# Gated attention and MLP for one token: the result in two PSUM banks, the MLP part added by matmul, one store, and the value products behind the second half of the scores

## The chip, the cores and the metric

The kernel runs on one core of a Trainium2 chip. Such a core has a matmul engine (TensorE, PE in the profile, with PEld for its weight loads), a vector engine (VectorE, DVE), a scalar engine (ScalarE, ACT), GpSimd (POOL) and SyncE (SP), which here issues most transfers. Matmuls write to PSUM; the other tiles lie in SBUF. The metric is the device time of one execution in microseconds, and kernels are compared by the median of several executions.

## The reference

One token for each of 8 sequences goes through a windowed attention over a cache (A) and an MLP (B), mixed by a gate per sequence:

```python
def _A_ref(x, k_cache, v_cache, wq, wo):            # x: 8 x 1 x 448
    W = 1024                                        # the last 1024 of 4096 positions
    q = (x @ wq) -> 8 x 16 heads x 1 x 256
    k, v = last W rows of 8 key/value heads, each used by 2 query heads
    p = softmax(q k^T / 16)
    return (p v).reshape(8, 1, 4096) @ wo           # wo: 4096 x 448
def _B_ref(x, w1, b1, w2, b2):
    return gelu(layernorm(x) @ w1 + b1) @ w2 + b2   # 448 -> 1792 -> 448
g = sigmoid((x * gate_w).sum(-1))                   # one number per sequence
return g * a + (1 - g) * b
```

Everything is bf16 in memory. Keys and values of the window are 33.5 MB each, and wo and wq 3.7 MB each; no part is read twice.

## The kernel before

The attention is cut into 16 units (`u`): one sequence and four of its eight key/value heads each, 2 MB of K and 2 MB of V. K and V of a unit, and the weights, come through a ring of nine SBUF slots. A list (`plan`) fixes the order of the loads: wq, K0, w1, w2, then K of a unit followed by V of two units before, last V14, V15 and the two halves of wo in ten pieces (`WO_PARTS`, L72, says how each of four quarters is cut). All of them are issued by SP in that order; `done` marks a slot as used and lets `pump` issue the next load into it.

The order of the work on each engine is the order in which the program is written (`manual_schedule`), so an instruction that waits holds up everything behind it on its engine. For a unit the steps are:

- `turn_keys` (L358, DVE, two halves): K is transposed in 32x32 blocks.
- `scores` (L424 and L430, PE, two halves): one masking matmul and eight matmuls into a PSUM tile `S`.
- `top` (L442, L444, DVE), `share` (L450, PE): the maximum, exchanged between the four heads.
- `expo` (L456 DVE, L459 ACT): exponentials `E` and their row sums.
- `turn` (L472, DVE): `E` transposed to `ET`. `total` (L483, PE) and `invert` (L493 DVE, L494 ACT): the inverse of the row sums.
- `values` (L502, PE): 16 matmuls of `ET` with V into `PO`, in four column groups, and a scaled copy of one half of `PO` on ACT (`first`, L511).
- `gather` (L517, DVE): the other half added, giving `os_`. `finish` (L532, PE): two f32 matmuls that transpose and normalise, and a copy into `oT` (L535, ACT).

The loop at L615 runs these steps for several units at once: in the round of unit `u` come the scores of `u`, the softmax of `u`-1, the value products of `u`-2 and the end of `u`-3. After the loop (L633 on) the remaining steps of the last units follow. `spread_rows` (L657 PE, L664 DVE) brings `oT` into the row order of wo, for two quarters at a time: the first two need units of the first heads, the others all units. `project` (L673) multiplies one quarter with wo: eight weight blocks, each used by three matmuls of 160, 144 and 144 output columns, which lie at partitions 0, 32 and 64 of one PSUM tile `A_ps`. `mlp_out` (L593 to L605) does the same for the MLP and leaves `(1 - g) * b` in `mixb` in that layout. At the end one DVE operation (L691) computes `g * a + mixb` for all three column parts, and three stores (L701) write them: two issued by SP and one by ACT.

Of the kernel before, what the change touches and what calls it, by code (L numbers as in the profile page):

```python
# [8 lines left out]
ACT = mybir.ActivationFunctionType  # L9
ALU = mybir.AluOpType  # L10
AXIS = mybir.AxisListType
BF16 = mybir.dt.bfloat16
F32 = mybir.dt.float32
# [5 lines left out]
def kernel(  # L19
# [15 lines left out]
    nc = tc.nc  # L35
    P = nc.NUM_PARTITIONS

    NB, Sq, D = A_x.shape
# [13 lines left out]
    NF = F // P  # L52
    FH = F // 2
    HH = HD // 2
    PAIR = 2
    OT = 4
    CUTS = (0, 160, 304, D)
    DO = CUTS[1]
    QN = 512
    QUAD = 4  # L60
    RQ = QUAD * rep
# [7 lines left out]
    HPQ = 4  # L69
    NHQ = Hq // HPQ  # L70
    NJ8 = HPQ * NJ
    WO_PARTS = [[(0, 4), (4, 8)]] * 2 + [[(0, 4), (4, 6), (6, 8)]] * 2  # L72
    RING = 9
    LAG = 2
    NK = 4
# [30 lines left out]
    def done(n=1):  # L106
        consumed[0] += n
        pump()
# [37 lines left out]
    def add_kv(name, src, u, parts=1):  # L146
        add((name, u), kv_loader(src, u, parts))
# [15 lines left out]
        if u >= LAG:  # L163
            add_kv("v", A_v_cache, u - LAG)
    for u in range(NQ - LAG, NQ):
        add_kv("v", A_v_cache, u)
    for q in range(0, NHQ, 2):
        add(
            ("wo", q),
# [9 lines left out]
    def slot(*key):  # L179
        return slots[index[key]]  # L180

    consts.tile([P, 304], BF16, name="pad")
    x_sb = consts.tile([NB, D], BF16)
    pump()
    nc.scalar.dma_start(x_sb[:], xf)
# [16 lines left out]

    NX = NR + 2

    def tiles(ps):
        return [
            (ps[32 * i : 32 * i + NB, 0 : c1 - c0], slice(c0, c1))
            for i, (c0, c1) in enumerate(zip(CUTS, CUTS[1:]))
        ]

    xz = consts.tile([NB, 2, P], BF16)
    yz = consts.tile([NB, 2, P], BF16)
    nc.vector.memset(xz[:], 0.0)
# [12 lines left out]
    place = consts.tile([P, CH, BLK], BF16)  # L226
    oT = consts.tile([P, Hq, NJ, NB], BF16)
    gg = consts.tile([NB, 2], F32)
    spread = consts.tile([NB, OT, P // OT], F32)
    gg_s = consts.tile([P, 2], F32)  # L230
    ones_r = consts.tile([1, NB], BF16)
    mixb = consts.tile([P, DO], F32)
    res = consts.tile([P, DO], BF16)
    nc.vector.memset(spread[:], 0.0)
    nc.vector.memset(ones_r[:], 1.0)

    def transposed(dst, src, srcz):
# [57 lines left out]
    def norm_and_gate():  # L295
        stats = consts.tile([NB, nc.vector.BN_STATS_DIM], F32)
        nc.vector.bn_stats(stats[:], x_sb[:])
        mv = consts.tile([NB, nc.vector.BN_AGGR_DIM], F32)
        nc.vector.bn_aggr(mv[:], stats[:])
        eps_t = consts.tile([NB, 1], F32)  # L300
        nc.vector.memset(eps_t[:], 1e-5)
        rstd = consts.tile([NB, 1], F32)
        nc.scalar.activation(rstd[:], mv[:, 1:2], ACT.Sqrt, bias=eps_t[:], scale=1.0)
        nc.vector.reciprocal(rstd[:], rstd[:])
        y_sb = consts.tile([NB, D], BF16)
        nc.vector.tensor_scalar(
            y_sb[:],
            x_sb[:],
            scalar1=mv[:, 0:1],
            scalar2=rstd[:],  # L310
            op0=ALU.subtract,
            op1=ALU.mult,
        )
        for h in range(2):
            nc.vector.tensor_copy(yz[:, h, h::2], y_sb[:, DM:D])
        transposed(yT, y_sb, yz)
        prod = consts.tile([NB, D], F32)
        gl = consts.tile([NB, 1], F32)
        nc.vector.scalar_tensor_tensor(
            prod[:],  # L320
            in0=x_sb[:],
            scalar=1.0,
            in1=gw_b[:],
            op0=ALU.mult,
            op1=ALU.mult,
            accum_out=gl[:],
        )
        gth = consts.tile([NB, 1], F32)
        nc.scalar.activation(gth[:], gl[:], ACT.Tanh, scale=0.5)
        nc.vector.tensor_scalar(  # L330
            gg[:, 0:1], gth[:], 0.5, 0.5, op0=ALU.mult, op1=ALU.add
        )
        nc.vector.tensor_scalar(
            gg[:, 1:2], gth[:], -0.5, 0.5, op0=ALU.mult, op1=ALU.add
        )
        nc.vector.tensor_copy(
            spread[:, :, 0:NB],
            ident[0:NB, 0:NB]
            .rearrange("p (o b) -> p o b", o=1)
            .to_broadcast([NB, OT, NB]),  # L340
        )
        gp = ps_misc.tile([P, 2], F32, tag="misc", name="gp")
        nc.tensor.matmul(  # L343
            gp[:],
            lhsT=spread[:].rearrange("p i b -> p (i b)"),
            rhs=gg[:],
            start=True,
            stop=True,
        )
        nc.vector.tensor_copy(gg_s[:], gp[:])  # L350

# [2 lines left out]
    def turn_keys(u, hf):  # L354
        kn = slot("k", u)
        kt = ktpool.tile([P, CH, NK, BLK, NPAR], BF16, tag="kt", name="kt")
        KT[u, hf] = kt
        nc.vector.transpose(  # L358
            kt[:].rearrange("p c k x r -> p (c k x r)").bitcast(WORD),
            kn[:, hf * CH * Dh : (hf + 1) * CH * Dh].bitcast(WORD),  # L360
        )
        if hf == NH - 1:
            done()
# [163 lines left out]
    def finish(u):  # L527
        b, half = divmod(u, Hkv // QUAD)
        os_, rs = soft.pop(u), rsel.pop(u)
        sm = ps_sm.tile([P, NJ, RQ], F32, tag="sm", name="fin")  # L530
        for j in range(NJ):
            nc.tensor.matmul(  # L532
                sm[:, j, :], lhsT=os_[:, j::NJ], rhs=rs[:], start=True, stop=True
            )
        nc.scalar.copy(  # L535
            oT[:, half * RQ : (half + 1) * RQ, :, b].rearrange("p h j -> p j h"), sm[:]
        )

    def mlp_hidden():
# [30 lines left out]
        )  # L570
        z2 = consts.tile([P, NF, NB], F32)
        nc.vector.tensor_tensor(z2[:], z[:], z[:], op=ALU.mult)
        uu = consts.tile([P, NF, NB], F32)
        nc.vector.tensor_scalar(
            uu[:], z2[:], 0.044715, 1.0, op0=ALU.mult, op1=ALU.add
        )
# [1 line left out]
        nc.vector.tensor_tensor(w_[:], uu[:], z[:], op=ALU.mult)  # L578
        th = consts.tile([P, NF, NB], F32)
        nc.scalar.activation(th[:], w_[:], ACT.Tanh, scale=0.7978845608028654)  # L580
        hh = consts.tile([P, NF, NB], F32)
        nc.vector.tensor_scalar(hh[:], th[:], 1.0, 0.5, op0=ALU.add, op1=ALU.mult)
        hs = consts.tile([P, NF, NB], BF16)
        nc.vector.tensor_tensor(hs[:], hh[:], z[:], op=ALU.mult)
        return hs

    def mlp_out(hs):
        bb = ps_misc.tile([P, DO], F32, tag="misc", name="bb")
        nc.vector.memset(bb[:], 0.0)
        for c in range(NF):  # L590
            w = slot("w2")
            for dst, cols in tiles(bb):
                nc.tensor.matmul(  # L593
                    dst,
                    lhsT=hs[:, c, :],
                    rhs=w[:, c * D + cols.start : c * D + cols.stop],
                    start=(c == 0),
                    stop=False,
                )
        for dst, cols in tiles(bb):  # L600
            nc.tensor.matmul(
                dst, lhsT=ones_r[:], rhs=b2_r[:, cols], start=False, stop=True
            )
        done()
        nc.scalar.activation(mixb[:], bb[:], ACT.Copy, scale=gg_s[:, 1:2])  # L605

    norm_and_gate()
    query()
# [6 lines left out]
    for u in range(1, NQ):  # L615
        turn_keys(u, 0)
        scores(u, 0)
        if u >= LAG + 1:
            gather(u - LAG - 1)
        if u >= LAG:  # L620
            turn(u - LAG)
            total(u - LAG)
        if u >= LAG + 1:
            finish(u - LAG - 1)
        top(u - 1)
        share(u - 1)
        turn_keys(u, 1)
        if u >= LAG:
            values(u - LAG)
            invert(u - LAG)  # L630
        scores(u, 1)
        expo(u - 1)
    u = NQ - 1  # L633
    A_ps = ps_misc.tile([P, DO], F32, tag="misc", name="A_ps")
    gather(u - 2)
    finish(u - 2)
    turn(u - 1)
    total(u - 1)
    values(u - 1)
    top(u)  # L640
    share(u)
    invert(u - 1)
    expo(u)
    gather(u - 1)
    finish(u - 1)
    turn(u)
    total(u)
    invert(u)
    nc.vector.memset(A_ps[:], 0.0)
    oP = consts.tile([P, NJ8, NHQ, NB], BF16)  # L650
    oTv = oT[:].rearrange("p (q i) j b -> p i j q b", i=HPQ)

    def spread_rows(q0, q1):
        pp = ps_sm.tile([P, HPQ, NJ, q1 - q0, NB], F32, tag="sm", name="pp")
# [13 lines left out]
    def project(q):  # L668
        w = slot("wo", q - q % 2)
        for j in range(NJ8):  # L670
            o = ((q % 2) * NJ8 + j) * D
            for dst, cols in tiles(A_ps):
                nc.tensor.matmul(  # L673
                    dst,
                    lhsT=oP[:, j, q, :],
                    rhs=w[:, o + cols.start : o + cols.stop],
                    start=(q == 0 and j == 0),
                    stop=(q == NHQ - 1 and j == NJ8 - 1),
                )

    HALF = NHQ // 2
    spread_rows(0, HALF)
    values(u)
    gather(u)
    finish(u)
    project(0)
    spread_rows(HALF, NHQ)
    for q in range(1, NHQ):
        project(q)

    nc.vector.scalar_tensor_tensor(  # L691
        res[:],
        in0=A_ps[:],
        scalar=gg_s[:, 0:1],
        in1=mixb[:],
        op0=ALU.mult,
        op1=ALU.add,
    )
    for i, (src, cols) in enumerate(tiles(res)):
        eng = nc.sync if i % 2 == 0 else nc.scalar  # L700
        eng.dma_start(out_f[:, cols], src)  # L701


# [28 lines left out]
```

## Time and profile before

| | |
|---|---|
| median of 6 runs | 190.43 us (190.25 to 190.6) |
| the profiled execution | 190.72 us |
| its span in the profile | 188.9 us |
| read from memory | 77.68 MB, 411 GB/s over the span |
| PE, DVE, ACT busy | 132.4, 127.9, 43.3 us |
| mean granted clock of PE | 0.889 |

The span runs from the first to the last instruction of the profiled execution; 1.8 us of its time lie outside the span. In the rows by slice the span is cut into 40 equal parts and each digit is a busy share in tenths; PEclk is the clock that PE was granted. In a timeline row stand the start, the duration of the group, the engine, the line, the operation, the tiles written and read, and the count; in brackets is the engine's idle time before it and what ended it. In a chain row stand the start and the length of a piece. In a row by stretch stand the stretch, its length, and for PE, PEld, DVE, ACT and POOL the busy time and count, then the granted clock, the DMA share and GB/s. A busy PE is not one at its peak, since matmuls overlap.

### The profile page before, as it was taken

To read this page: it belongs to the slowest core of one execution; us is meant where nothing else is said; L and a number is where in the kernel's file an instruction comes from. 1 tells how busy PE (TensorE), PEld (TensorE's weight loads), DVE (VectorE), ACT (ScalarE), POOL (GpSimd) and SP (SyncE) were. 2 spreads that over 40 slices of the span, in tenths; PEclk is the share of its full clock that TensorE was granted. 3 is DMA by queue.
4 is the path that set the end of the run, shared out by engine and by line. 5 is a ranking of instruction groups with operands and counts; after the bars stand their busy time and mean duration, and the time that the engine had idled before them with its cause. 6 is when DMAs were issued, how large, how long until landed. Compare 5 with 4: busy or idle time off the path is not lost.

```text
span 188.9 us, 2411 instructions
## 1 busy us (share of the span) xinstructions
PE 132.4 (70%) x966; PEld 69.7 (37%) x975; DVE 127.9 (68%) x186; ACT 43.3 (23%) x91; POOL 5.0 (3%) x7
## 2 busy tenths in 40 slices
PE   0056979797848984767867686857299839987582
PEld 0022853442415342423332253333153415354471
DVE  7840488998949494949494949494767777686300
ACT  2032310034130404040404040404004400415400
POOL 8100000000000000000000000000000000000000
PEclk9999999999996699996999799999957975699855
DMA  6999999999999999999999999999999999999990
GB/s 213 414 425 433 439 422 428 437 434 416 434 434 434 430 430 430 427 434 430 430 434 421 434 427 437 430 430 434 427 430 430 434 427 441 413 441 422 406 369 22
DMA packets 7293, 77.84 MB, mean 412 GB/s; under 512 B 993, under 2 KB 1650, under 8 KB 2546
## 3 DMA queue, kind: packets, MB, share of 16 engines
q1 hardware_dynamic: 7088, 77.67, 96.9%
q8 instruction: 7, 0.11, 0.2%
q10 hardware_dynamic: 194, 0.02, 0.1%
q14 instruction: 4, 0.03, 0.0%
HBM read 77.68 MB, written 0.01 MB: 411 GB/s over the span
## 4 chain that ended last, share of the span: by engine, by line
DMA 79%; DVE 10%; PE 6%; ACT 2%; issue 1%; SPq 0%; ACTq 0%
DMA slot<-in_A_k_cache_dram 39%; DMA slot<-in_A_wo_dram 20%; DMA slot<-in_A_v_cache_dram 20%; DVE kt L358 4%; PE Sq L372 2%; PE S L430 2%; DVE xz L246 1%; ACT qw L413 1%; DVE qw L415 1%; PE qt L387 1%; ACT qs L382 1%; PE qp L400 1%; DVE Sq L199 0%; PE fin L532 0%; PE gp L343 0%
## 5 line engine op out<-in xcount | busy, mean ns | idle before, releaser
L358 DVE STREAM_TRANSPOSE kt<-slot 128x2048 int32<-128x2048 int32 x32 | 73.7, 2305 | 32.1 <-DMA slot<-in_A_k_cache_dram 32.1
L430 PE MATMUL S<-kt,qw 128*128 128x512 bf16 x256 | 70.0, 420 | 32.1 <-DVE kt L358 27.5
L430 PEld LDWEIGHTS <-qw 128*128 128x128 bf16 x256 | 26.4, 103 | 69.4 <-issue 48.2
L459 ACT ACTIVATE E<-S,nmx 128x1024 bf16<-128x1024 f32 x16 | 22.2, 1389 | 3.5 <-DVE nmx L456 3.5
L535 ACT CAST oT<-fin 128x16 bf16<-128x16 f32 x16 | 3.6, 227 | 76.2 <-PE fin L532 76.2
L502 PE MATMUL PO<-slot,ET 128*16 128x512 bf16 x256 | 19.2, 426 | 0.4 <-DVE ET L472 0.2
L442 DVE TENSOR_REDUCE mx<-S 128x1 f32<-128x1024 f32 x16 | 19.0, 1185 | 0.0
L511 ACT ACTIVATE first<-PO,own 128x256 f32<-128x256 f32 x16 | 7.6, 475 | 28.5 <-PE PO L502 28.5
L472 DVE STREAM_TRANSPOSE ET<-E 128x512 int32<-128x512 int32 x16 | 11.2, 698 | 2.2 <-ACT E L459 2.2
L450 PE MATMUL mz<-m,same 128*128 128x4 f32 x32 | 6.6, 278 | 4.5 <-ACT oT L535 4.1
L424 PE MATMUL S<-place,foreign 128*128 128x512 bf16 x23 | 9.6, 419 | 0.1
L483 PEld LDWEIGHTS den<-rowsum,rowden 128*128 128x128 f32 x32 | 7.0, 223 | 3.7 <-issue 1.4
L450 PEld LDWEIGHTS mz<-m,same 128*128 128x128 f32 x32 | 5.4, 211 | 6.4 <-ACT oT L535 5.3
L502 PEld LDWEIGHTS <-ET 128*16 128x16 bf16 x256 | 5.3, 92 | 5.4 <-issue 1.7
L424 PEld LDWEIGHTS <-foreign 128*128 128x128 bf16 x32 | 3.2, 101 | 9.4 <-issue 7.6
L673 PE MATMUL A_ps<-slot,oP 128*8 128x144 bf16 (+1 forms) x96 | 5.2, 319 | 0.9 <-DMA slot<-in_A_wo_dram 0.7
L483 PE MATMUL den<-rowsum,rowden 128*128 128x1 f32 x32 | 5.2, 231 | 0.4 <-ACT E L459 0.4
L415 DVE CAST qw<-qp 32x512 bf16<-32x512 f32 x4 | 2.8, 688 | 3.4 <-ACT qw L413 3.4
L494 ACT ACTIVATE rsel<-sel,rb 128x8 f32<-128x8 f32 x16 | 4.7, 296 | 1.1 <-DVE rb L493 1.1
L293 POOL MEMSET qw<- 128x5120 bf16 x1 | 4.4, 4365 | 0.0
L391 DVE COPY qd<-qt 128x64 bf16<-128x64 bf16 x4 | 0.6, 218 | 5.5 <-PE qt L387 5.5
L673 PEld LDWEIGHTS <-oP 128*8 128x8 bf16 x96 | 3.6, 109 | 1.9 <-issue 1.7
(135 smaller groups left out, 88.2 us busy)
## 6 DMA issues: line engine op xcount, KB each, us to landing
slot<-in_A_v_cache_dram SPq DMA_DIRECT2D x16, 2048.0 KB, 37.1
slot<-in_A_k_cache_dram SPq DMA_DIRECT2D x15, 2048.0 KB, 36.6
slot<-in_A_wo_dram SPq DMA_DIRECT2D x6, 448.0 KB, 31.3
slot<-in_A_wq_dram SPq DMA_DIRECT2D x1, 2048.0 KB, 7.7
slot<-in_A_k_cache_dram SPq DMA_DIRECT2D x2, 1024.0 KB
slot<-in_B_w_dram SPq DMA_DIRECT2D x1, 1568.0 KB
slot<-in_B_w_dram SPq DMA_DIRECT2D x1, 1344.0 KB, 11.8
slot<-in_A_wq_dram SPq DMA_DIRECT2D x1, 1024.0 KB
```

The costliest lines, as they stand in the source:

```text
L358: nc.vector.transpose(kt[:].rearrange("p c k x r -> p (c k x r)").bitcast(WORD), kn[:, hf * CH * Dh : (hf + 1) * CH * Dh].bitcast(WORD),)
L424: nc.tensor.matmul(S[u][:, cols], lhsT=foreign[:], rhs=place[:], start=True, stop=False)
L430: nc.tensor.matmul(S[u][:, cols], lhsT=qw[:, j, u, m * RQ : m * RQ + P], rhs=kt[:, :, k, :, par], start=False, stop=(k == NK - 1 and par = ...
L442: nc.vector.reduce_max(mx[:], S[u][:], axis=AXIS.X)
L450: nc.tensor.matmul(mz[:], lhsT=same[:], rhs=m4[:], start=True, stop=True)
L459: nc.scalar.activation(E[:].rearrange("p c x i -> p c i x"), S.pop(u)[:].rearrange("p (c i x) -> p c i x", i=PAIR, x=BLK), ACT.Exp, bias=n ...
L472: nc.vector.transpose(ET[:].rearrange("p c r i -> p (c r i)").bitcast(WORD), E[:].rearrange("p c x i -> p (c x i)").bitcast(WORD),)
L483: nc.tensor.matmul(den[u][:], lhsT=rowden[:], rhs=rowsum[:], start=True, stop=True)
L494: nc.scalar.activation(rsel[u][:], sel2[:], ACT.Copy, scale=rb[:])
L502: nc.tensor.matmul(PO[32 * t : 32 * t + PAIR * RQ], lhsT=ET[:, c, 0:RQ, :], rhs=vn[:, PAIR * c * Dh : PAIR * (c + 1) * Dh], start=(c < QUA ...
L511: nc.scalar.activation(first[:], PO[:, 0, :], ACT.Copy, scale=own[:, 0:1])
L673: nc.tensor.matmul(dst, lhsT=oP[:, j, q, :], rhs=w[:, o + cols.start : o + cols.stop], start=(q == 0 and j == 0), stop=(q == NHQ - 1 and j ...
```

## The change

Seven things are edited.

1. In the loop, `values` and `invert` of unit `u`-2 come after `scores(u, 1)` and `expo(u-1)`, not before them.
2. The result is no longer one tile in three column parts but two PSUM tiles of 224 columns each, `A_lo` at partitions 0 to 7 and `A_hi` at partitions 32 to 39 of a former scores tile. `project` runs two matmuls of 224 columns for each weight block.
3. The MLP output is computed in one part of 448 columns (14 matmuls and the bias), scaled by `1 - g` into `mixb`.
4. `begin` puts `mixb` into the two result tiles by f32 matmuls with an identity; the projection adds to that. It stands between `finish(u-1)` and `turn(u)` of the last unit.
5. The gate multiplies in `finish`: its copy into `oT` takes a scale for each sequence (`gg_s`, now 128x8, made by a matmul with ones). The end needs only two copies, one on DVE and one on ACT, and a single store.
6. V15 is loaded in two parts, and the last piece of wo in two.
7. At the end, quarter 0 is projected before `finish` of the last unit, and quarter 1 before the second `spread_rows`.

Smaller edits save SBUF: `uu` and `hh` reuse tiles, and the padding changes.

```diff
-    WO_PARTS = [[(0, 4), (4, 8)]] * 2 + [[(0, 4), (4, 6), (6, 8)]] * 2
+    WO_PARTS = [[(0, 4), (4, 8)]] * 2 + [
+        [(0, 4), (4, 6), (6, 8)],
+        [(0, 4), (4, 6), (6, 7), (7, 8)],
+    ]
...
-        add_kv("v", A_v_cache, u)
+        add_kv("v", A_v_cache, u, parts=2 if u == NQ - 1 else 1)
...
+        nc.vector.memset(each[:], 1.0)
+        nc.vector.tensor_scalar_mul(each[:, 0:NB], ident[0:NB, 0:NB], gg[:, 0:1])
+        gp = ps_misc.tile([P, NB], F32, tag="misc", name="gp")
         nc.tensor.matmul(
+            gp[:], lhsT=each[:, NB : NB + P], rhs=each[:, 0:NB], start=True, stop=True
         )
...
-        nc.scalar.copy(
-            oT[:, half * RQ : (half + 1) * RQ, :, b].rearrange("p h j -> p j h"), sm[:]
+        nc.scalar.activation(
+            oT[:, half * RQ : (half + 1) * RQ, :, b].rearrange("p h j -> p j h"),
+            sm[:],
+            ACT.Copy,
+            scale=gg_s[:, b : b + 1],
         )
...
+        bb = ps_misc.tile([NB, D], F32, tag="misc", name="bb")
+        w = slot("w2")
         for c in range(NF):
             nc.tensor.matmul(
+                bb[:],
+                lhsT=hs[:, c, :],
+                rhs=w[:, c * D : (c + 1) * D],
+                start=(c == 0),
+                stop=False,
             )
+        nc.tensor.matmul(bb[:], lhsT=ones_r[:], rhs=b2_r[:], start=False, stop=True)
         done()
-        nc.scalar.activation(mixb[:], bb[:], ACT.Copy, scale=gg_s[:, 1:2])
+        nc.scalar.activation(mixb[:], bb[:], ACT.Copy, scale=gg[:, 1:2])
...
         turn_keys(u, 1)
+        scores(u, 1)
+        expo(u - 1)
         if u >= LAG:
             values(u - LAG)
             invert(u - LAG)
-        scores(u, 1)
-        expo(u - 1)
...
+    A_lo = ps_misc.tile([NB, DH2], F32, tag="misc", name="A_lo")
+    A_hi = ps_s.tile([P, W], F32, tag="S", name="A_hi")
+    halves = (A_lo[:], A_hi[32 : 32 + NB, 0:DH2])
...
+    def begin():
+        for i, dst in enumerate(halves):
+            nc.tensor.matmul(
+                dst,
+                lhsT=ident_f[:],
+                rhs=mixb[:, i * DH2 : (i + 1) * DH2],
+                start=True,
+                stop=False,
+                skip_group_check=True,
+            )
...
-            for dst, cols in tiles(A_ps):
+            for i, dst in enumerate(halves):
                 nc.tensor.matmul(
                     dst,
                     lhsT=oP[:, j, q, :],
-                    rhs=w[:, o + cols.start : o + cols.stop],
-                    start=(q == 0 and j == 0),
+                    rhs=w[:, o + i * DH2 : o + (i + 1) * DH2],
+                    start=False,
                     stop=(q == NHQ - 1 and j == NJ8 - 1),
+                    skip_group_check=True,
                 )
...
+    finish(u - 1)
+    begin()
+    turn(u)
+    total(u)
+    invert(u)
     spread_rows(0, HALF)
     values(u)
     gather(u)
+    project(0)
     finish(u)
-    project(0)
+    project(1)
     spread_rows(HALF, NHQ)
-    for q in range(1, NHQ):
+    for q in range(HALF, NHQ):
         project(q)
-    nc.vector.scalar_tensor_tensor(
-        res[:],
-        in0=A_ps[:],
-        scalar=gg_s[:, 0:1],
-        in1=mixb[:],
-        op0=ALU.mult,
-        op1=ALU.add,
-    )
-    for i, (src, cols) in enumerate(tiles(res)):
-        eng = nc.sync if i % 2 == 0 else nc.scalar
-        eng.dma_start(out_f[:, cols], src)
+    nc.vector.tensor_copy(res[:, 0:DH2], halves[0])
+    nc.scalar.copy(res[:, DH2:D], halves[1])
+    nc.sync.dma_start(out_f, res[:])
```

## The prediction

> **What bounds the kernel now.** The page comes first. Its rows by slice show that the transfers never pause between the first and the last slice, while no engine is full.
>
> ```profile
> PE   0056979797848984767867686857299839987582
> DVE  7840488998949494949494949494767777686300
> PEclk9999999999996699996999799999957975699855
> DMA  6999999999999999999999999999999999999990
> ```
>
> So up to about 184 us, work is free as long as it doesn't hold up a transfer; only the end can change the time. I read that from the chain of waits of the last 30 us.
>
> ```profile
> 178.90 6.65 DMA slot<-in_A_wo_dram
> 185.55 0.04 issue
> 185.59 0.46 PE A_ps L673 x4
> 186.05 0.03 issue
> 186.07 0.38 DVE res L691
> ```
>
> The last piece of wo lands at 185.55, four recorded matmuls and one DVE operation follow, and the stores take the rest of the 188.9. The timeline then tells how much room the engines had before that landing.
>
> ```profile
> 166.73 2.31 DVE L358 STREAM_TRANSPOSE kt<-slot 128x2048 int32<-128x2048 int32 x1
> ...
> 168.42 1.04 PE L502 MATMUL PO<-slot,ET 128*16 128x512 bf16 x16
> ...
> 169.62 1.91 PE L430 MATMUL S<-kt,qw 128*128 128x512 bf16 x8 [0.16 <-issue]
> ...
> 170.02 0.48 DVE L517 SCALAR_TENSOR_TENSOR os__1446<-PO,own,first 128x256 f32<-128x256 f32 x1 [0.88 <-ACT first L511]
> ...
> 171.55 0.71 DVE L472 STREAM_TRANSPOSE ET<-E 128x512 int32<-128x512 int32 x1 [1.05 <-ACT E L459]
> ...
> 175.91 0.71 DVE L472 STREAM_TRANSPOSE ET<-E 128x512 int32<-128x512 int32 x1 [1.18 <-ACT E L459]
> ...
> 176.78 1.04 PE L502 MATMUL PO<-slot,ET 128*16 128x512 bf16 x16 [0.21 <-DMA slot<-in_A_v_cache_dram]
> ...
> 178.98 1.02 PE L532 MATMUL fin<-rsel,os__1541 128*128 128x8 f32 x4 [1.15 <-DVE os__1541 L517]
> 179.93 1.23 PE L673 MATMUL A_ps<-slot,oP 128*8 128x160 bf16 x24
> ...
> 181.11 2.73 PE L673 MATMUL A_ps<-slot,oP 128*8 128x144 bf16 x48
> ...
> 184.51 1.51 PE L673 MATMUL A_ps<-slot,oP 128*8 128x160 bf16 x24 [0.67 <-DMA slot<-in_A_wo_dram]
> ```
>
> Two margins are to be seen. The turned weights of the last unit (units are numbered 0 to 15) are ready at 175.91 + 0.71 = 176.62, and V15 lands at 176.76: the chain of small steps after K15 has 0.14 us to spare. After that the projection runs just ahead of wo, with 0.67 us of waiting in front of its last quarter. Last, the granted clock by stretch:
>
> ```profile
> 171.00:174.40 3.40, 2.50 (x27) 1.48 (x25) 2.34 (x6) 1.41 (x5) 0.00 (x0) 1.00 0.95 409
> 174.40:177.80 3.40, 2.27 (x38) 1.49 (x38) 1.47 (x5) 1.86 (x4) 0.00 (x0) 1.00 0.99 408
> 177.80:181.20 3.40, 2.25 (x54) 2.19 (x53) 0.48 (x1) 0.70 (x2) 0.00 (x0) 0.50 1.03 410
> 181.20:184.60 3.40, 2.63 (x66) 1.92 (x52) 0.29 (x1) 0.00 (x0) 0.00 (x0) 0.50 0.86 332
> ```
>
> The seventh number is the granted share: from 177.8 to the end PE runs at half clock, although it is 2.63 of 3.4 us busy in the last stretch.
>
> **Cost, part by part.** The profiled execution took 190.72 us for a span of 188.9, 0.29 above the median of 190.43. I sum on its own time and take off 0.29 at the end.
>
> *Value products behind the second half of the scores.* Inside the loop this is free: DVE waits 1.6 to 2.7 us for K in each of the last three iterations. V slots are released about 2.5 us later, but a V load lands a median 37.1 us after its issue; SP's queue, where the next K load stands behind that V load, stays far ahead. At the end there is no next K to wait for. Unit 15's scores now start when its keys are turned, 169.04, and end at 169.07 + 1.91 = 170.98. Only then does PE take the value products of unit 13, 1.04, to 171.95 (168.42 to 169.46 before). ACT's scaled copy (0.47) and the hand-overs bring the DVE operation of L517 from 170.02 to 172.51. DVE runs in order, and queued behind it are the turn of unit 14, the maximum of unit 15 and with it the exponential and turn of unit 15. The turn of unit 14 moves from 171.55 to about 172.9: 1.35 later, though its exponential is done 0.8 earlier. The rest of the chain keeps its durations, so ET of unit 15 is ready at 177.98, and its value products start at 178.05 in place of 176.78: +1.27. V15's landing no longer decides, and its split into two parts (two SP issues of 0.53 us instead of one) gains nothing.
>
> *Projection.* Before, a weight block is used by three matmuls of at most 160 columns in three column groups; after, by two of 224. At half clock 24 matmuls took 1.23 us: 154 ns per block. The scores' row at half clock, eight of 512 columns in 3.57 us, gives 446 ns per 512 columns; 224 columns cost 195 ns, or 1.56 us per quarter. Scaling the 1.23 by 224/160 gives 1.72. I take 1.62 between them. At full clock the MLP's row (42 matmuls in 1.13, 81 ns per block of three) plus 64 columns at 238 ns per 512 gives 111 ns, 0.89 per quarter.
> The Trainium skill, in "TensorE: Matmul & The Clock Gate", section "Back-to-back issue gap", has N/1.2 ns per matmul at the cold clock. For 224 columns that is 187 ns, an estimated 1.49 per quarter; by it the forecast would be 0.5 us lower, and for 160 columns it gives 133 where the row has 154.
>
> *Order at the end.* The first quarter now fills the PE wait for L517 (177.82 to 178.98 before): good for one quarter of work. But the second spread of rows now stands between quarters 1 and 2 with nothing behind it that PE may do. Its 16 matmuls take 0.34, and the DVE copy with hand-overs 0.46 (0.29 of copy, 0.12 before it, 0.05 after).
>
> *Sum at half clock.* Values 178.05 + 1.88 (the row of unit 12 at half clock) = 179.93; quarter 0 to 181.55; the two f32 products of L532, 1.02, to 182.57; quarter 1 to 184.19; spread and copy 0.80 to 184.99; quarters 2 and 3 to 188.23. All of wo has landed by then. PE ends 2.18 later than its 186.05. PE is now the bound, not DMA.
>
> *MLP part and gate on PE.* Two f32 matmuls of 224 columns start the banks, between L532 of unit 14 and the row sums of unit 15. No row has such a shape. From below: two record pairs in different column groups at the bf16 rate, 0.2 us. From above: four records one after the other at four times that rate, 1.66. PE waits there from about 176.96 to the end of the exponential at 177.38, so up to 0.42 is hidden; I take 0.4, as L532's f32 pairs (0.61 for four records, mostly weight loads) lie nearer the low end, and keep +1.2 for the range. The scale in L535's copy costs the difference of L494's 0.29 to its 0.23, 0.06, which lies beside PE work except ahead of the first spread. MLP output without column tiles: 14 matmuls of 448 columns at 208 ns, 2.9 instead of 1.13 us, at 33 us. Its cover is the compute's waiting for K from 45 us on; without that it would cost 1.8. Gate setup, memsets and the changed padding lie at the start or off the path: nothing.
>
> *Transfers.* In the packet records a packet of 8192 bytes takes 309 ns against 611 for 16384, and 896 bytes 41 against 74 for 1792. V15 in halves and the last wo piece in halves are 8 more packets per engine each: 0.06 + 0.06 us later landing, 185.67. It matters only if DMA stays the bound.
>
> *Result and store.* DVE 0.38 for 160 columns is replaced by DVE and ACT side by side, 224 columns each. ACT's casts of 16 and of 512 columns take 0.23 and 0.58, so about 0.38: no change. Of the three stores, SP issued two, the second after 0.37 us, and its packets were the last, 0.37 behind the first ones. One store saves 0.37.
>
> Total: +2.18 - 0.37 = +1.81, so 192.53 on its own time and 192.24 against the median. A change under 0.2% (0.38 us) can't be told from none.
>
> **Rivals.**
> *Full clock at the end (faster, or on the edge of it).* Then values end at 179.1, quarter 0 at 180.0, L532 waits for its operand to 180.2 and ends at 180.8, quarter 1 at 181.7, spread and copy at 182.3, and quarters 2 and 3 wait for wo as now. PE ends at 185.67 + 0.04 + 0.25 = 185.96: -0.09 - 0.37 = -0.46, 190.0. It decides if PE ends before 186.4, which takes full clock by about 182. For it: values and quarter 0 are 3.5 us of unbroken PE work, and full clock returned at 164.2 after an unbroken 3.4. Against: 2.63 of 3.4 busy brought nothing back, and between the values of units 14 and 15 lie now some 3 us of small products alone, which is poorer than the stretch that lost the clock at 177.8.
> The same page of the Trainium skill, section "Part 1: The HAM clock gate (the "warmup" mystery)", says that an idle window of about 3.4 us halves the clock and a busy one restores it, with windows that run free of the kernel. By this rule a busy window that happened to fit would give this rival's 190.0, and a misfit the 192.2; that the trace keeps half clock through a mostly busy stretch fits it.
>
> *Half clock in unit 14's second scores too.* Before, that stretch (157.3 to 164.2) was at half clock and cost nothing. Now the values of unit 12 stand behind those scores: they would end about 165.3, DVE's L517 for unit 12 would start at 165.84, not 164.38, and 1.45 more is lost: 193.7. Against: the values now fill the PE gap of 2.99 us ahead of unit 14 in which the clock fell.
>
> *The delay doesn't arise.* If L517 of unit 13 kept its time, values would start at 176.78; quarter 0, held by the wo piece landing at 178.9, ends about 179.7, and the steps above end at 186.4: +0.34 - 0.37, no change, 190.4. Only the order of the DVE queue speaks against it, and it speaks clearly.
>
> **Numbers.** Likeliest 0.68; full clock 0.14; unit 14 late too 0.11; no delay 0.07. The likeliest's own range is 191.2 (values still at full clock, -0.84; quarters at 1.56, -0.24) to 193.4 (the f32 start uncovered, +1.2, the rest as summed). The whole range, 190.2 to 193.9, takes in the last two rivals and leaves out most of the full clock case and the likeliest's ends. Faster 0.10 (most of the full clock case), same 0.11 (the rest of it, and no delay), slower 0.79.
>
> **What the profile after would show.** L517's DVE operation of unit 13 waiting for ACT until about 172.5; unit 15's value products started by DVE's turn, not by V15, near 178; no PE wait for wo in the last quarter; the chain ending in projection matmuls of PE for 6 us or more; half clock there; one store. I am wrong if the last quarter still waits for wo, or if the clock is full from 182 on; a clock that differs between executions would also spread the times.

## The result and the profile after

The changed kernel takes 192.46 us at the median of 17 executions, the kernel before 190.38 of 35 beside it: 1.1% slower. The ratio is 1.0075 with a 95% interval of 1.0053 to 1.0096; it leaves out six executions of the changed kernel that lie more than 1.5% above its fastest (193.55 to 194.82) and that the median counts, since their mean granted clocks (0.857 to 0.884) lie with those of the executions from 191.9 to 193.4 (0.857 to 0.882). The spread is as much a part of the result as the median: the executions lie between 190.53 and 194.82, while nearly all of the kernel before lie between 190.1 and 190.6. The clock goes with it: the four executions under 191.0 have a mean granted clock of 0.900 to 0.908, the other thirteen of 0.857 to 0.884.

The execution that was profiled is the fastest of them, 190.53 us with a span of 188.7. It has to be read with that in mind: it shows the delay, and how a clock that came back in time hid it; no slower execution of this kernel was profiled. The code moved, so L430, L442, L502 and L517 of before are L418, L430, L490 and L505 here; the new `begin` is L628, the projection L657. The timeline of the changed kernel from the last keys on:

```profile
166.35 2.30 DVE L346 STREAM_TRANSPOSE kt<-slot 128x2048 int32<-128x2048 int32 x1
...
168.71 1.90 PE L418 MATMUL S<-kt,qw 128*128 128x512 bf16 x8 [1.04 <-DVE nmx L444]
...
170.53 1.04 PE L490 MATMUL PO<-slot,ET 128*16 128x512 bf16 x16
...
172.19 0.48 DVE L505 SCALAR_TENSOR_TENSOR os__1419<-PO,own,first 128x256 f32<-128x256 f32 x1 [3.42 <-ACT first L499]
172.59 0.70 DVE L460 STREAM_TRANSPOSE ET<-E 128x512 int32<-128x512 int32 x1
...
177.02 0.54 PE L628 MATMUL A_lo<-mixb,ident_f 8*8 8x224 f32 x1
...
177.06 0.71 DVE L460 STREAM_TRANSPOSE ET<-E 128x512 int32<-128x512 int32 x1 [1.11 <-ACT E L447]
...
177.87 0.59 PE L471 MATMUL den<-rowsum,rowden 128*128 128x1 f32 x2
178.38 0.34 PE L641 MATMUL pp<-oT,ident 128*32 128x32 bf16 x15
...
178.55 1.89 PE L490 MATMUL PO<-slot,ET 128*16 128x512 bf16 x15
...
183.88 0.26 PE L657 MATMUL A_lo<-slot,oP 128*8 128x224 bf16 x1 [0.42 <-DVE oP L648]
...
185.22 0.26 PE L657 MATMUL A_lo<-slot,oP 128*8 128x224 bf16 x1
...
185.49 0.26 PE L657 MATMUL A_lo<-slot,oP 128*8 128x224 bf16 x1
```

The value products of unit 13 (170.53) now stand behind the scores of unit 15 (168.71). DVE's L505 waits 3.42 us for what comes of them, and the turn of unit 14 is queued behind it: 172.59, with keys that were ready 0.4 us earlier than in the profile of before, where it stood at 171.55. ET of unit 15 is ready at 177.77 instead of 176.62, and no transfer is waited for there any more. The last rows are the surprise: in this execution PE has caught up. The last piece of wo, issued at 179.84 and 5.60 us on its way, landed at 185.44, and the last weight block starts at 185.49, 0.27 us behind the block before it where the others are 0.09 apart. So the last block waits for wo as before; its matmuls end 0.27 us earlier than in the profile of before. The granted clock by stretch (the seventh number) says how:

```profile
174.85:178.27 3.42, 2.68 (x12) 1.85 (x12) 1.26 (x3) 2.25 (x5) 0.00 (x0) 0.50 1.01 413
178.27:181.68 3.41, 3.41 (x49) 1.89 (x49) 0.94 (x3) 0.77 (x2) 0.00 (x0) 0.50 1.03 410
181.68:185.10 3.42, 3.00 (x66) 2.67 (x64) 0.29 (x1) 0.33 (x1) 0.00 (x0) 1.00 0.76 280
```

One stretch of 3.41 us was filled with small products, the value products and the first quarter, and the clock came back at 181.68. The three quarters after it then took half the time of the first. Where the clock doesn't come back, PE should still be at work after wo has landed; that is argued for this kernel, and seen in the profile of a kernel with the same loop order below. The chain of work that the profile follows back from the end runs, over its last ten microseconds, through PE; the short wait for wo at 185.49 is not in it:

```profile
178.72 1.72 PE PO L490 x16
...
181.86 0.57 PE fin L520 x4
...
183.53 0.30 DVE oP L648
...
185.49 0.26 PE A_lo L657
185.79 0.37 DVE res L692
```

### The profile page after: what moved, and what is told of

Read it like the earlier page. It is cut to its first block, busy times and chain, and to the rows that moved or that the text cites. A ratio compares the mean times of both kernels' runs of the same rounds, so it can differ in the third digit from the quotient of the medians.

```text
span 188.7 us, 2305 instructions
## 1 busy us (share of the span) xinstructions
PE 136.7 (72%) x909; PEld 66.2 (35%) x917; DVE 128.9 (68%) x185; ACT 46.7 (25%) x92; POOL 5.0 (3%) x7
## 4 chain that ended last, share of the span: by engine, by line
DMA 58%; PE 20%; DVE 18%; ACT 2%; issue 1%; ACTq 0%
DMA slot<-in_A_k_cache_dram 58%; PE S L418 8%; DVE kt L346 7%; PE PO L490 3%; DVE mx L430 2%; PE A_lo L657 2%; PE Sq L360 2%; DVE ident_f L230 2%; DVE ET L460 1%; PE fin L520 1%; PE mz L438 1%; PE qt L375 1%; ACT qs L370 1%; ACT first L499 1%; PE qp L388 1%
## 5 line engine op out<-in xcount | busy, mean ns | idle before, releaser
L418 PE MATMUL S<-kt,qw 128*128 128x512 bf16 x256 | 72.4, 431 | 27.3 <-DVE nmx L444 19.3
L418 PEld LDWEIGHTS <-qw 128*128 128x128 bf16 x256 | 26.7, 104 | 63.6 <-issue 44.3
L490 PE MATMUL PO<-slot,ET 128*16 128x512 bf16 x256 | 20.8, 455 | 0.0
L430 DVE TENSOR_REDUCE mx<-S 128x1 f32<-128x1024 f32 x16 | 19.0, 1186 | 0.0
L523 ACT ACTIVATE oT<-fin,gg_s 128x16 bf16<-128x16 f32 x16 | 5.3, 328 | 36.7 <-PE fin L520 36.6
L490 PEld LDWEIGHTS <-ET 128*16 128x16 bf16 x256 | 5.6, 97 | 14.4 <-issue 12.2
L471 PEld LDWEIGHTS den<-rowsum,rowden 128*128 128x128 f32 x32 | 6.3, 204 | 3.1 <-ACT oT L523 0.7
L412 PEld LDWEIGHTS <-foreign 128*128 128x128 bf16 x32 | 4.5, 141 | 7.4 <-issue 7.2
L657 PE MATMUL A_lo<-slot,oP 128*8 128x224 bf16 x32 | 4.4, 291 | 0.4 <-DVE oP L648 0.4
L657 PE MATMUL A_hi<-slot,oP 128*8 128x224 bf16 x32 | 4.4, 291 | 0.0
```

The source lines that it names most:

```text
L412: nc.tensor.matmul(S[u][:, cols], lhsT=foreign[:], rhs=place[:], start=True, stop=False)
L418: nc.tensor.matmul(S[u][:, cols], lhsT=qw[:, j, u, m * RQ : m * RQ + P], rhs=kt[:, :, k, :, par], start=False, stop=(k == NK - 1 and par = ...
L430: nc.vector.reduce_max(mx[:], S[u][:], axis=AXIS.X)
L471: nc.tensor.matmul(den[u][:], lhsT=rowden[:], rhs=rowsum[:], start=True, stop=True)
L490: nc.tensor.matmul(PO[32 * t : 32 * t + PAIR * RQ], lhsT=ET[:, c, 0:RQ, :], rhs=vn[:, PAIR * c * Dh : PAIR * (c + 1) * Dh], start=(c < QUA ...
L523: nc.scalar.activation(oT[:, half * RQ : (half + 1) * RQ, :, b].rearrange("p h j -> p j h"), sm[:], ACT.Copy, scale=gg_s[:, b : b + 1],)
```

## The experiments

The theory going in: the new order of the loop delays the end of the last units by more than the slack there, and the half clock at the end turns the delay into time. The rivals: the new projection costs it, or the order costs it through something else than the clock.

**The order of the loop put back.**

```diff
         turn_keys(u, 1)
-        scores(u, 1)
-        expo(u - 1)
         if u >= LAG:
             values(u - LAG)
             invert(u - LAG)
+        scores(u, 1)
+        expo(u - 1)
```

> The changed kernel with the order of the loop put back: values and invert before the second half of the scores, all else as changed. Theory (the chain after the last K, then the clock): the turn of the last unit is ready near 176.6 again and V15 decides, so the median falls to 190.0 to 190.8 us and the executions lie within about 0.5 us of each other. Rival (the new projection: two matmuls of 224 columns, and the second spread between quarters 1 and 2): the median stays at 192 or more and spread as wide as the changed kernel's, 190.5 to 194.8.

190.64 us at the median, 190.34 to 191.17; ratio to before 1.0013 (1.0003 to 1.0023). In this kernel L505 of unit 13, the turn of unit 14 and the value products of unit 15 stand 1.0 to 1.2 us earlier than before the change:

```profile
168.86 0.48 DVE L505 SCALAR_TENSOR_TENSOR os__1419<-PO,own,first 128x256 f32<-128x256 f32 x1 [0.19 <-ACT first L499]
170.37 0.71 DVE L460 STREAM_TRANSPOSE ET<-E 128x512 int32<-128x512 int32 x1 [1.03 <-ACT E L447]
...
175.76 1.89 PE L490 MATMUL PO<-slot,ET 128*16 128x512 bf16 x15
```

L505 of unit 13 is 3.3 us earlier than in the changed kernel, the value products of unit 15 2.8 us. Nearly all of the loss, 1.8 of 2.1 us at the median, lies in the moved lines. The projection, the MLP part and the store together leave 0.2 us in this order. And PE was at half clock here, from 174.22 to 184.47:

```profile
177.63:181.05 3.42, 3.25 (x33) 2.17 (x28) 0.48 (x1) 0.80 (x2) 0.00 (x0) 0.50 1.03 412
181.05:184.47 3.42, 2.87 (x46) 1.88 (x42) 0.29 (x1) 0.00 (x0) 0.00 (x0) 0.50 0.91 342
```

Still the last block starts at 185.48, 0.04 us after the last piece of wo (185.44): half clock without the delay leaves the end to the transfer.

**The order alone, in the kernel before.**

```diff
         turn_keys(u, 1)
+        scores(u, 1)
+        expo(u - 1)
         if u >= LAG:
             values(u - LAG)
             invert(u - LAG)
-        scores(u, 1)
-        expo(u - 1)
```

> The kernel before with one edit: values and invert behind the second half of the scores and the exponential. Theory: the value products of the last unit start 1.3 us later than 176.78; the old projection is 0.35 to 0.4 us per quarter cheaper at half clock and the second spread is covered, so 190.5 to 193 with a median near 191.5, and executions spread over 2 us or more. Rival (the projection is at fault): no change, 190.4, and a narrow spread.

192.86 us, 192.79 to 193.44 in four executions; ratio 1.0127 (1.0111 to 1.0142). Alone it costs at least as much as the whole change, and 1.4 us more than the middle of what was expected. The rest of the change may be of some use under the delay, as quarter 0 ahead of the last finish fills a wait; four executions don't show that. The timeline, of the slowest of the four, shows a term that the theory lacked:

```profile
168.92 3.40 PE L430 MATMUL S<-kt,qw 128*128 128x512 bf16 x8 [1.22 <-DVE nmx L456]
...
172.25 1.16 PE L502 MATMUL PO<-slot,ET 128*16 128x512 bf16 x16
...
174.04 0.48 DVE L517 SCALAR_TENSOR_TENSOR os__1446<-PO,own,first 128x256 f32<-128x256 f32 x1 [5.05 <-ACT first L511]
...
179.83 1.89 PE L502 MATMUL PO<-slot,ET 128*16 128x512 bf16 x16
```

The scores of unit 15 ran at half clock here, 3.40 us in place of 1.90, and since the value products of unit 13 now wait for them, L517 came 1.5 us later still.

**The old order in the last round alone.**

```diff
         turn_keys(u, 1)
+        late = u < NQ - 1
+        if u >= LAG and not late:
+            values(u - LAG)
+            invert(u - LAG)
         scores(u, 1)
         expo(u - 1)
-        if u >= LAG:
+        if u >= LAG and late:
             values(u - LAG)
             invert(u - LAG)
```

> The changed kernel with the old order in the last round of the loop alone (unit 15); rounds 2 to 14 keep the new order. Theory: inside the loop the order is free and only the last round counts, so the same as with the old order throughout: 190.0 to 190.8 us, narrow. Rival (the new order harms in every round, by lowering the clock or by accumulating): 191.5 or more, with a wide spread.

190.76 us at the median; ratio 1.0012 (1.0003 to 1.0022). Nine of eleven executions lie between 190.38 and 190.87, two at 193.92 and 194.03. In most executions, then, the order in rounds 2 to 14 is free and the last round alone counts. What happened in the two others wasn't profiled. Half clock in the scores of unit 14, with the value products of unit 12 behind them, would delay the last round in this way; that is argued, not shown.

**PE kept busy.** Nine matmuls that nobody reads, put where PE waits after the loop.

```diff
+    def fill(n):
+        for _ in range(n):
+            nc.tensor.matmul(
+                A_hi[:, QN:W], lhsT=foreign[:], rhs=place[:], start=True, stop=True
+            )
+
     HALF = NHQ // 2
+    fill(4)
     gather(u - 2)
...
     values(u - 1)
+    fill(1)
     top(u)
     share(u)
+    fill(3)
     invert(u - 1)
...
     total(u)
+    fill(1)
     invert(u)
```

> The changed kernel with nine matmuls more that nobody reads (128x512, into the unused second bank of A_hi), put where PE waits after the loop: four ahead of the first finish, one after the values of unit 14, three after share of unit 15, one after total of unit 15. Theory (the half clock at the end is what the 1.3 us of delay turn into 2 us and a wide spread): the clock stays full from 171 on, PE keeps up with wo, and the median is 189.8 to 190.6 with executions within 0.7 us. Rival (the clock doesn't matter, the order alone costs it): 192 or more, since the nine matmuls can only add work.

190.55 us, 190.38 to 190.84; ratio 1.0004 (0.9996 to 1.0013). The spread is gone with the loss, though the order is that of the changed kernel and, in this profile, the value products of unit 15 start at 179.81, 1.26 us later than in the changed kernel's profile. By stretch:

```profile
170.20:173.60 3.40, 3.40 (x21) 0.69 (x18) 0.00 (x0) 0.56 (x2) 0.00 (x0) 0.50 1.00 422
173.60:177.00 3.40, 3.11 (x32) 1.54 (x28) 2.51 (x5) 1.16 (x4) 0.00 (x0) 1.00 1.01 416
177.00:180.40 3.40, 3.33 (x45) 1.84 (x48) 1.61 (x5) 2.46 (x6) 0.00 (x0) 1.00 1.03 416
180.40:183.80 3.40, 2.88 (x64) 2.23 (x52) 0.53 (x2) 0.81 (x2) 0.00 (x0) 1.00 1.01 389
183.80:186.20 2.40, 2.02 (x32) 1.42 (x32) 0.27 (x2) 0.00 (x0) 0.00 (x0) 1.00 0.21 70
```

The clock came back at 173.6, before the first unread matmul, and stayed full through the small steps, where the changed kernel lost it (174.85). The four quarters and the last finish then keep up with wo: its last piece landed at 185.85, and the last block starts at 185.89. This is what tells the delay from its price: delay and half clock together cost 2 us, each alone (here the delay, with the old order the half clock) next to nothing.

**The same filling with the old order, and in the kernel before.** The first has five unread matmuls (1, 3 and 1 at the last three places above), the second ten (1, 3, 2 behind the finish of unit 14, 4 behind the values of unit 15; a spare scores tile takes them).

> The changed kernel with the old order of the loop and five unread matmuls of 512 columns where PE waits after the loop (one after the values of unit 14, three after share of unit 15, one after total of unit 15). Theory (chain and clock together): the clock stays full more often, the last piece of wo decides, 190.2 to 190.5 us with executions within 0.5 us, a little under the 190.64 of the old order alone. Rival (what is left above the kernel before is not the clock but the projection or the split loads): 190.6 or more, as without the five.

190.49 us, 190.28 to 190.68; ratio 1.0002 (0.999 to 1.0014).

> The kernel before with ten unread matmuls of 512 columns where PE waits after the loop (one, three, two, and four after the values of unit 15). Theory: the kernel before is bound by wo's landing, so a full clock at the end saves only what follows the last landing, 0.1 to 0.2 us: 190.2 to 190.4. Rival (half clock at the end costs it too): 190.0 or less. If the filling itself delays the steps it stands among: 190.6 or more.

190.63 us, 190.37 to 191.69; ratio 1.0019 (1.0006 to 1.0032). With the old order the five make the executions lie closer (0.4 us, from 0.8). The kernel before gains nothing from a fuller clock, as a kernel does that waits for wo; the ten matmuls cost it 0.2 us at the median. Two of twelve executions lie at 191.5 and 191.7, but their spans are 189.1 and 188.7, so most of what they take longer lies outside the span. No version beats the kernel before by more than a measurement can tell.

**`begin` moved to where PE waits.**

```diff
+    begin()
     gather(u - 2)
     finish(u - 2)
...
     finish(u - 1)
-    begin()
     turn(u)
```

> The changed kernel with begin (the two f32 matmuls that put the MLP part into the result banks) straight after the loop, where PE waits for DVE, and not between the last finish steps. Theory: in the profile of the changed kernel begin held the row sums, the spread and so the value products of unit 15 by 0.7 us at half clock; moved, the median falls by 0.4 to 1.0 us to 191.4 to 192.1, still with a wide spread. Rival (begin is covered, the delay is that of DVE's queue alone): unchanged within 0.3 us of 192.4.

191.56 us, 190.49 to 192.02 in six executions; ratio 1.0059 (1.0039 to 1.0079). The median is 0.9 us lower, the upper end of what was expected, but the ratios, 1.0059 and 1.0075, differ by 0.3 us and their intervals overlap: six executions don't settle the size. That `begin` was on the path is shown by the timeline of the changed kernel: the row sums of unit 15 stand behind it, from 177.02 to 177.87, with their exponential done at 177.02.

**The last softmax ahead of the late gather.**

```diff
-    gather(u - 2)
-    finish(u - 2)
     turn(u - 1)
     total(u - 1)
-    values(u - 1)
     top(u)
     share(u)
     invert(u - 1)
     expo(u)
+    gather(u - 2)
+    finish(u - 2)
+    values(u - 1)
     gather(u - 1)
```

> The changed kernel, its loop order kept; after the loop the steps stand in another order: turn and total of unit 14, top and share of unit 15, invert of unit 14, expo of unit 15, and only then gather and finish of unit 13, values, gather and finish of unit 14, begin. So DVE has no operation ahead of turn of unit 14 that waits for the late value products. Theory (the step that costs is DVE's operation of L517 queued ahead of the last softmax): the turn of unit 15 is ready near 175, before V15 lands at 176.8, and the median falls to 190.2 to 190.8 us. Rival (the value products behind the scores cost through PE itself): 191.5 or more.

192.11 us, 191.72 to 194.51; ratio 1.0109 (1.0068 to 1.015). This theory fell. Its timeline:

```profile
173.67 1.42 ACT L447 ACTIVATE E<-S,nmx 128x1024 bf16<-128x1024 f32 x1 [0.27 <-DVE nmx L444]
...
174.66 1.04 PE L490 MATMUL PO<-slot,ET 128*16 128x512 bf16 x16
...
176.25 0.48 DVE L505 SCALAR_TENSOR_TENSOR os__1462<-PO,own,first 128x256 f32<-128x256 f32 x1 [2.28 <-ACT first L499]
176.65 0.70 DVE L460 STREAM_TRANSPOSE ET<-E 128x512 int32<-128x512 int32 x1
...
178.88 1.89 PE L490 MATMUL PO<-slot,ET 128*16 128x512 bf16 x15
```

The last exponential starts 1.9 us earlier than in the changed kernel, and yet the value products of unit 15 start 0.3 later. By the rows, the late values of unit 13 hold a second chain: through the single `PO` tile to the values of unit 14, their gather and finish, and the spread that stands ahead of the values of unit 15. In the order that was tried, the turn of unit 15 stands on DVE behind the gather of that chain too, and `begin` still ahead of the spread. The profile also shows what half clock to the end looks like:

```profile
177.31:180.72 3.41, 3.41 (x43) 1.56 (x44) 0.50 (x3) 0.63 (x2) 0.00 (x0) 0.50 1.03 416
180.72:184.14 3.42, 3.42 (x36) 2.55 (x30) 0.48 (x1) 0.80 (x2) 0.00 (x0) 0.50 0.98 374
184.14:187.55 3.41, 2.95 (x48) 2.11 (x46) 0.29 (x1) 0.00 (x0) 0.00 (x0) 0.50 0.11 35
```

The last piece of wo landed at 185.51 here; PE works on to 188.12, in the order of the changed kernel's last steps.

**Both moves.** The two edits above in one kernel.

> The changed kernel's loop order with both moves after the loop: the last softmax ahead of gather of unit 13 (that alone: 192.11 us), and begin straight after the loop (that alone: 191.56). Theory (behind the late values of unit 13 stand two chains, the last softmax and the one through the single PO tile, values, gather and finish of unit 14, spread; the later one decides): with the softmax early the PO chain decides, the value products of unit 15 start near 178.1, 0.7 to 1.1 earlier than with either move alone, and the median is 190.8 to 191.4. Rival (the softmax order is without effect and begin alone counts): 191.5, as with begin moved alone. Rival (only the softmax counted and was masked by begin): 190.2 to 190.6, V15's landing decides.

192.86 us, 191.56 to 194.38; ratio 1.0123 (1.0075 to 1.0171). At the median none of the three expectations came true: three executions near 191.7 and three near 194. In the profiled one the scores of unit 15 ran at half clock (3.37 us), which puts the steps behind them 1.5 us later, and the value products of unit 15 start at 180.28. What the three near 194 have in common was not profiled; their mean clock, 0.867, is that of the others (0.856 to 0.865) or above it. Which of the two chains decides at equal clocks stays open.

**A second store, and a longer list of PE instructions.** One store instead of three had been counted as 0.37 us saved, and with the old order back nothing of it was to be seen. The store was tried in the kernel with the old order and the five unread matmuls.

```diff
-    nc.sync.dma_start(out_f, res[:])
+    nc.sync.dma_start(out_f[:, 0:DH2], res[:, 0:DH2])
+    nc.sync.dma_start(out_f[:, DH2:D], res[:, DH2:D])
```

> The changed kernel with the old loop order and the five unread matmuls (190.49 us), its result written by two stores of 224 columns, both issued by SP, in place of one. Theory formed from the profiles (2.4 to 2.5 us lie between the first store's issue and the end, with one store as with three, so the closing steps and not the number of stores set the end): 190.3 to 190.7 us, unchanged. Rival (a second store on SP costs 0.37 us, and the saving of the change was used up elsewhere): 190.8 to 190.95.

191.09 us, 190.7 to 191.34; ratio 1.0028 (1.0018 to 1.0037); 0.6 more than with one store at the median, 0.5 by the ratios. The theory that the number of stores doesn't matter fell: a second store does cost what it was said to, or more. The saving is lost behind the store. SP's waits at the end, first of the kernel before, then of the changed one (in total, times, longest):

```profile
SPq L727 <- DMA out_dram<-res: 0.7, 3, 0.4
SPq L727 <- PEq L727: 0.6, 2, 0.4
```

```profile
SPq L720 <- PEq L720: 0.9, 2, 0.7
SPq L720 <- DMA out_dram<-res: 0.7, 1, 0.7
```

In the closing steps, SP waits 0.7 us for PE's queue where it waited 0.4. From the start of the last packet of the result to the end pass 1.54 us after the change and 1.20 before. Two lengths of PE's list were tried on top of the old order and the five unread matmuls, with 16 and 40 unread matmuls of 8 columns at the very start.

> The changed kernel with the old loop order and the five unread matmuls (190.49 us), and 16 unread matmuls of 8 columns more on PE at the very start, where it waits for x. They cost no time there; they only make PE's instruction list longer. Theory (in the changed kernels the closing steps wait 0.7 us for PE's queue where the kernel before has 0.4, because PE then fetches instructions, so it hangs on the length of its list): for one of the two lengths the wait falls to 0.4 and the median by 0.3 us, to 190.2. Rival (the wait has nothing to do with the list's length): 0.7 and 190.5 for both.

> The same with 40 unread matmuls at the start. Theory: as for 16, at another length; at least one of the two shows the shorter wait of 0.4 us and 190.2. Rival: 0.7 and 190.5 for both.

190.58 us, ratio 0.9996 (0.998 to 1.0012), and 190.67, ratio 1.0001 (0.9988 to 1.0014). The wait is 0.7 in both, so these two lengths don't decide. Among the kernels with the changed projection it was 0.4 in the two with the last softmax moved ahead, and 0.7 in all others. What makes it stays open.

## Why the prediction was right, step by step

The forecast was 192.2 us for a measured 192.46, and the mechanism behind it held: with the order put back the loss went, with the order alone it came, and with a full clock the delay cost nothing.

- *L517 of unit 13 and what is queued behind it.* 172.51 forecast, 172.19 measured; turn of unit 14 at 172.9 and 172.59; ET of unit 15 ready at 177.98 and 177.77. Right within about 0.3 us, and the keys were ready 0.4 earlier in this profile. That only DVE's queue speaks for the delay was too narrow: without it the chain through `PO` brings a like delay.
- *Free inside the loop.* Held in nine of eleven executions with the last round alone put back.
- *V15 in two parts gains nothing.* True under the new order. With the old one its second part lands at 176.30, as SP's next issue tells, and the value products start at 175.76, 0.5 us ahead of it; no run shows that this is worth time.
- *Two f32 matmuls, 0.4 us, covered.* Mis-sized. They took 0.91 us at half clock (177.02 to 177.93) and 0.54 at full clock in the filled kernel, and held up row sums, spread and values: unit 15's value products start at 178.55, 0.5 later than forecast and 0.7 later than `ET` would have let them. Both bounds, 0.2 and 1.66, had been worked out at the full clock rate (238 ns per 512 columns) for a stretch that the sum has at half clock. Moving the two matmuls was worth 0.3 to 0.9 us, which six executions don't settle. The +1.2 kept for the range had held it.
- *A quarter of the projection, 1.62 us at half clock.* Too dear. The blocks start 187 ns apart at half clock (180.19 to 181.50 for eight), 1.50 per quarter, and 95 ns at full clock, 0.76 in place of 0.89. The Trainium skill ("TensorE: Matmul & The Clock Gate", section "Back-to-back issue gap") has N/1.2 ns per matmul at the cold clock, an estimated 187 for 224 columns; the trace agrees, and here the rule was better than the scaled row.
- *Second spread with nothing behind it, 0.80.* Measured 183.12 to 183.88, 0.76, at full clock.
- *Half clock to the end.* Not true of the one execution profiled, which is the full clock rival: 190.0 forecast, 190.53 measured. Its condition held as put: PE was at full clock by 182 and ended before 186.4, and both signs named for being wrong are there, the full clock and a last quarter that waits for wo. Its chance of 0.14 was low; 4 of 17 executions lie under 191.0. That the others ran at half clock to the end is argued from their lower mean clocks and from the kernel with the last softmax moved, where PE ended at 188.12 against 188.23 in the sum.
- *Half clock in unit 14's scores* was priced. The same in unit 15's scores, 3.4 us in place of 1.9, was not, and the kernel with the order alone, the one with `begin` moved and the one with both moves show it in their profiles. It could raise the upper end by 1.5 us: six executions of 17 are above 193.4, the likeliest case's upper bound, and three above 193.9. Whether these had it, or the same in unit 14's, wasn't profiled.
- *One store, -0.37.* The term is right in itself and was given back by the closing steps: from the first store's issue to the end 2.41 us before, 2.47 after.

So two errors of about 0.5 us (f32 start, quarters) have opposite signs, the store took back 0.37, and the forecast hit the middle of a distribution that it had only half described. The direction and the cause were worked out; that the median came within 0.3 us is in part luck.

## What to carry to other kernels

In a kernel bound by transfers, a reordering that is free in every round can still cost in the last one, where no next load covers it: follow each in-order queue from the last transfer back, with the slack in numbers. Ask also at what clock PE will be in that stretch; here a chain of small steps lost the clock just before the dense work, and then the dense work behind a delay takes about twice its time. If executions of one kernel differ by 2% while its neighbour's agree, look at the clock of the stretch before looking for contention, and don't read one profile as the median.

## What was not expected of the hardware

The clock changed only at steps of 3.41 us: in the changed kernel's profile it fell at 174.85 and rose two steps later, at 181.68; in that of before it rose at 164.17 and fell four steps later, at 177.82. The steps lie elsewhere against the same work from one profile to the next: with the same loop, in which the last keys are ready within 0.6 us of each other, the last fall came at 174.85 in the changed kernel, 175.60 with `begin` moved and 177.31 with the last softmax moved. That they also move from one execution of a kernel to the next would explain 190.5 to 194.8 us, and is argued, not shown. How busy PE was in a stretch didn't tell what the clock did behind it. Stretches with 2.50 (before) and 3.00 (changed) busy kept a full clock, and one with 2.63 didn't bring it back; the one with 3.41 that did has a counterpart in the kernel with the last softmax moved, where 3.41 and 3.42 didn't, and with the old order one with 2.87 did (181.05 to 184.47). What in a stretch counts stays open. Nine matmuls of no use removed nearly all of the spread and 1.9 us of the median. And a store fewer on a queue, which another kernel shows to be worth 0.5 to 0.6 us, can vanish in the closing steps of the program.
